# Attention into two expert layers: fills and first weight splits taken off GpSimd, and shorter block lookups

## The chip, the cores and the metric

The kernel runs on one core of one Trainium2 chip. The metric is the device time of one execution in microseconds (us). The five engines are named as in the profile: PE is TensorE's matmul and PEld its weight load, DVE is VectorE, ACT is ScalarE, POOL is GpSimd, and SP is the queue that issues most of the DMAs.

## The reference

Chunked attention (8 batches, 8 heads, 576 positions, chunks of 64), whose output is read as 4608 tokens of 512 numbers, then a layer of 8 experts that picks one expert per token, then a second layer of 8 experts with a capacity of 576 tokens each.

```python
def _attn_ref(q, k, v):
    scores = scale * np.matmul(q_c, k_c.transpose(0, 1, 2, 4, 3))
    scores = scores - np.max(scores, axis=-1, keepdims=True)
    attn = np.exp(scores)
    attn = attn / (np.sum(attn, axis=-1, keepdims=True) + 1e-09)
    out = np.matmul(attn, v_c)

def _moe_ref(x, w_gate, w_output_gate, w1, w2):
    e_idx = np.argmax(x @ w_gate, axis=1)
    for e in range(E):
        mask = e_idx == e
        h = np.maximum(x[mask] @ w1[e], 0.0)
        out[mask] = gate_w[mask, None] * eom[mask, e, None] * (h @ w2[e])
...
    x = _moe_ref(x=x, **moe_kwargs)
    return _moe2_ref(x=x, **moe2_kwargs)
```

## The kernel before, in words

The program has three stages that run into one another. The attention stage (`attention`) works through NT = 36 tiles of 128 tokens. Tile t needs one transfer pair `load_qkv(t)` into one of NQ = 7 buffers `qkv0` to `qkv6`, each half of which must hold zeros, because the two chunks of a tile share one block-diagonal matmul; `blanks` writes those zeros once, before the first load into a buffer. For each tile, `scores` makes 16 small matmuls (L412), takes the row maximum `mx` on DVE (L416) and scales it to `nm` (L419); `exps` makes 8 ACT instructions (L426); `probs_T` transposes on PE (L433) and evicts on ACT (`eT`, L435); `values` makes 16 matmuls into `O` (L448), and DVE divides by the row sums (`rs`, `x`, L450 to L458). `x_T` and `logits` feed the gate of the first expert layer (`xT`, L470, and L479).

Every four tiles, the gate's logits of a group of 512 tokens are ready, and a generator `route(g)` (L494 to L600) is queued. It is a chain of some 25 short DVE steps with a little PE and ACT work: it finds each token's expert and its rank among the tokens of that expert, and looks up in a table `tab` [expert, block] which block of 256 slots holds that rank. The lookup is `jd`, `ge`, `lk`, `te` and `slot` (L564 to L589), over all NJ = 18 possible blocks of all 8 experts: `lk` is 4 x 18 x 8 = 576 elements per partition. Four indirect DMAs on POOL (L594) then scatter the tokens into a list. `advance` takes steps of the oldest route at fixed places between the attention's own instructions (9 steps per tile), so the route's DVE steps lie in the same in-order queue as `mx`, `nm`, `rs` and `x`. For groups 3, 4 and 5 the route is followed by `early`, some 15 more short DVE steps that choose a first block of the expert layer.

The order on PE, DVE, ACT and SP is the order in which the code issues; POOL's order is the scheduler's. At the start, DVE and POOL fill the first buffers, POOL makes the constants (`ident`, several iotas), then POOL fills the remaining buffers 4 to 6 (L388, L389) and 13 working tiles (L328). From tile T0 = 23 on, at every second tile, SP fetches one of four chunks of the first expert's weights into `raw[c]` (`wr`), and from T1 = 24 on POOL splits it into a rounded part `whi` (L368) and a rest `wlo` (L369), 1024 elements per partition each. Later splits, of all other weights, are made by `split` on ACT (`whi`, L711) and DVE (`wlo`, L712).

The second stage is the jobs of the first expert layer (256 to 512 tokens each, `layer1`, `layer2`), the third the second layer (`moe2`). The rest of the routes of the last groups is taken between the matmuls of the first two jobs.

Of the kernel before, what the change touches and what calls it, by code (L numbers as in the profile page):

```python
# [8 lines left out]
F32 = mybir.dt.float32  # L9
# [4 lines left out]
AF = mybir.ActivationFunctionType  # L14
OP = mybir.AluOpType
# [13 lines left out]
E = 8  # L29
F = 1024  # L30
NT = N // 128
G = 4
NG = NT // G
BT = 256
NB = (N + E * (BT - 1)) // BT
NJ = N // BT
# [24 lines left out]
T0, T1, T2 = 23, 24, 28  # L61
# [11 lines left out]
class Kernel:  # L73
# [5 lines left out]
    def constants(self):  # L79
# [35 lines left out]
        self.wgs = c.tile([128, 4, 32], F32, name="wgs")  # L115
        nc.vector.memset(self.wgs, 0.0)
        nc.scalar.dma_start(self.wgs[:, :, 0:2 * E], self.wg)
        self.wg2s = c.tile([128, 4, 32], F32, name="wg2s")
        nc.vector.memset(self.wg2s, 0.0)
        nc.scalar.dma_start(self.wg2s[:, :, 0:E], self.wg2)  # L120
# [90 lines left out]
    def setup(self, st):  # L211
# [29 lines left out]
        self.tab = fix.tile([128, E, NJ], F32, name="tab")  # L241
# [59 lines left out]
    def attention(self, st):  # L301
# [7 lines left out]
        self.blanks(0, nc.vector, nc.gpsimd)  # L309
        self.load_qkv(0)  # L310
        self.blanks(1, nc.gpsimd, nc.vector)
# [4 lines left out]
        spare = self.wk.tile([128, 1], F32, name="spare", bufs=1)  # L316
        nc.vector.memset(spare, 0.0)
        nc.scalar.activation(spare, spare, AF.Exp)
        self.constants()
        for i in range(4, NQ):  # L320
            self.blanks(i, nc.gpsimd, nc.gpsimd)
            if i < LOOK:
                self.load_qkv(i)
        opened, total, acc = self.opened0, self.total0, self.acc0
        self.state = (acc, opened, total)
        for a, v in ((self.tab, 0.0), (self.order, 0.0), (opened, 0.0), (total, 0.0), (acc, 0.0),
                     (self.L, 0.0), (self.blank, 0.0), (self.left, E * (E - 1) / 2), (self.C, 0.0), (self.first, 0.0), (self.m, -BIG), (self.f, -BIG), (self.dead, -BIG)):
            nc.gpsimd.memset(a, v)  # L328
# [8 lines left out]
        for t in range(NT):  # L337
# [48 lines left out]
    def blanks(self, i, left, right):  # L386
        a = self.qkvb[i]
        right.memset(a[:, QKV:], 0.0)  # L388
        left.memset(a[:, 0:QKV - 512], 0.0)  # L389
# [108 lines left out]
    def route(self, g, lg):  # L498
# [64 lines left out]
        jd = wk.tile([128, G, NJ], F32, name="jd")  # L563
# [896 lines left out]
```

## Time and profile before

| quantity | value |
|---|---|
| time, median of 3 runs | 1234.52 us (1226.85 to 1237.56) |
| the profiled execution, its own time | 1218.32 us |
| its span in the trace | 1216.5 us |
| PE busy | 1106.5 us (91%) |
| DVE busy | 780.2 us (64%) |
| ACT busy | 489.5 us (40%) |
| POOL busy | 201.2 us (17%) |

The busy shares are means over stages with different limits. The attention stage fills about the first 185 us; the first expert layer goes on to about 730 us. The profiled execution is faster than each of the three runs shown. A busy PE in this table is also a slow PE: its granted clock has two levels, 1.2 and 2.4 GHz, which views by stretch show as a mean between 0.5 and 1.0.

### The profile page before, as it was taken

How to read it: one execution, taken by the hardware profiler on the slowest of the kernel's cores; microseconds unless marked ns; L12 is line 12 of the kernel's file. 1: busy time of each engine (PE TensorE's matmuls, PEld its weight loads, DVE VectorE, ACT ScalarE, POOL GpSimd, SP SyncE). 2: the span in 40 equal slices, each digit the busy share in tenths (PEclk: the TensorE clock that was granted, in tenths of full speed). 3: DMA queues.
4: the chain of work that ended last, by engine and by line, in shares of the span. 5: the costliest groups of instructions: out<-in, count | busy, mean ns of one | idle time of the engine just before them, and what ended most of it. 6: DMA issues, size and time to landing. Idle time of an engine off the chain costs nothing.

```text
span 1216.5 us, 23354 instructions
## 1 busy us (share of the span) xinstructions
PE 1106.5 (91%) x8424; PEld 968.1 (80%) x8424; DVE 780.2 (64%) x2214; ACT 489.5 (40%) x1052; POOL 201.2 (17%) x242
## 2 busy tenths in 40 slices
PE   5988779899999997999899628999999999999997
PEld 4766559897898997999889618787878787889795
DVE  5867877865356455666666677778878787843330
ACT  4766645444244333444445304233333333333331
POOL 6022442211101110010001010122120212221101
PEclk9999989899999999999999857999999999999999
DMA  6977846785464566576677523243333334342401
GB/s 235 302 206 214 300 117 164 165 243 168 117 181 130 174 191 188 139 220 193 189 237 219 167 62 120 91 131 116 106 127 96 126 96 126 107 147 108 169 10 39
DMA packets 90554, 189.67 MB, mean 156 GB/s; under 512 B 22992, under 2 KB 46608, under 8 KB 90384
## 3 DMA queue, kind: packets, MB, share of 16 engines
q1 hardware_dynamic: 77904, 153.96, 42.6%
q0 software_dynamic: 11136, 32.59, 8.6%
q8 instruction: 77, 1.26, 0.4%
q10 hardware_dynamic: 1344, 1.10, 0.3%
q14 instruction: 93, 0.76, 0.2%
HBM read 152.33 MB, written 35.28 MB: 154 GB/s over the span
## 4 chain that ended last, share of the span: by engine, by line
PE 53%; issue 13%; DVE 7%; DMA 5%; POOL 2%; ACT 1%; SPq 1%; POOLq 0%; DVEq 0%; ACTq 0%
PE ph L879 6%; PE O L879 6%; PE ph L1326 4%; PE ph L1328 4%; PE ph L1330 4%; PE py L1363 3%; PE py L1361 3%; PE py L1365 3%; PE ph L902 2%; PE ph L904 2%; PE ph L903 2%; PE py L1348 2%; PE O L902 2%; PE O L903 2%; PE O L904 2%
## 5 line engine op out<-in xcount | busy, mean ns | idle before, releaser
L712 DVE TENSOR_TENSOR wlo<-wr,whi 128x1024 fp32r<-128x1024 f32 x122 | 146.8, 1222 | 43.0 <-ACT whi L711 41.3
L1326 PE MATMUL ph<-xhi,whi 128*128 128x256 f32 (+1 forms) x512 | 155.0, 303 | 3.6 <-ACT xhi L1296 2.6
L711 ACT ACTIVATE whi<-wr 128x1024 fp32r<-128x1024 f32 x122 | 126.0, 1054 | 76.1 <-DMA wr<-in_w_dram 39.6
L1328 PE MATMUL ph<-xlo,whi 128*128 128x256 f32 (+1 forms) x512 | 154.0, 301 | 0.0
L1330 PE MATMUL ph<-xhi,wlo 128*128 128x256 f32 (+1 forms) x512 | 153.9, 301 | 0.0
L853 POOL DMA_INDIRECT xr<-xs,idx x48 | 48.1, 1003 | 401.4 <-DVE idx L851 160.9
L1363 PE MATMUL py<-wlo,hhi 128*128 128x512 f32 x256 | 105.3, 411 | 0.0
L1334 ACT ACTIVATE hhi<-ph 128x256 fp32r<-128x256 f32 x128 | 49.1, 384 | 135.5 <-PE ph L1330 133.8
L1365 PE MATMUL py<-whi,hlo 128*128 128x512 f32 x256 | 103.0, 402 | 0.0
L1361 PE MATMUL py<-whi,hhi 128*128 128x512 f32 x256 | 102.7, 401 | 0.0
L1326 PEld LDWEIGHTS ph<-xhi,whi 128*128 128x128 f32 x512 | 98.0, 191 | 5.3 <-ACT xhi L1296 3.3
L1328 PEld LDWEIGHTS ph<-xlo,whi 128*128 128x128 f32 x512 | 98.0, 191 | 0.4 <-DVE xlo L1297 0.2
L1330 PEld LDWEIGHTS ph<-xhi,wlo 128*128 128x128 f32 x512 | 97.8, 191 | 0.0
L1282 DVE TENSOR_TENSOR wlo<-wr,whi 128x512 fp32r<-128x512 f32 x124 | 82.1, 685 | 8.4 <-ACT whi L1277 8.4
L1335 DVE SCALAR_TENSOR_TENSOR hlo<-ph,hhi 128x256 fp32r<-128x256 f32 x128 | 52.9, 420 | 49.6 <-ACT hhi L1334 30.6
L879 PE MATMUL O<-xhi,whi 128*128 128x256 f32 (+4 forms) x240 | 75.6, 318 | 7.1 <-issue 7.1
L879 PE MATMUL ph<-xhi,whi 128*128 128x256 f32 (+4 forms) x240 | 74.6, 317 | 3.6 <-issue 2.1
L426 ACT ACTIVATE ex<-ph,nm 128x64 f32<-128x64 f32 x288 | 68.5, 352 | 22.3 <-DVE mx L416 13.5
L879 PE MATMUL O<-xhi,wlo 128*128 128x256 f32 (+4 forms) x240 | 74.2, 313 | 0.4 <-issue 0.4
L879 PE MATMUL ph<-xhi,wlo 128*128 128x256 f32 (+4 forms) x240 | 73.1, 310 | 0.0
L879 PE MATMUL O<-xlo,whi 128*128 128x256 f32 (+4 forms) x240 | 71.2, 314 | 0.2 <-issue 0.2
L879 PE MATMUL ph<-xlo,whi 128*128 128x256 f32 (+4 forms) x240 | 68.8, 313 | 1.7 <-issue 1.7
(326 smaller groups left out, 2752.8 us busy)
## 6 DMA issues: line engine op xcount, KB each, us to landing
wr<-in_w_dram SPq DMA_DIRECT2D x128, 512.0 KB
qkv<-in_qkv_dram SPq DMA_DIRECT2D x72, 386.0 KB
wr<-in_w2b_dram SPq DMA_DIRECT2D x32, 512.0 KB
wr<-in_w1b_dram SPq DMA_DIRECT2D x30, 512.0 KB
x<-y SPq DMA_DIRECT2D x184, 64.0 KB
xs<-x SPq DMA_DIRECT2D x35, 256.0 KB
x<-blank SPq DMA_DIRECT2D x8, 514.0 KB
wr<-in_w1b_dram ACTq DMA_DIRECT2D x2, 512.0 KB
```

Source lines behind the costliest of these rows:

```text
L426: self.nc.scalar.activation(ex8[:, h // 2, h % 2, :], S8[:, h, :], AF.Exp, scale=0.125, bias=nm[:, h:h + 1])
L711: nc.scalar.activation(hi, self.raw[c], AF.Copy)
L712: (eng or nc.vector).tensor_tensor(lo, self.raw[c], hi.bitcast(F32), op=OP.subtract)
L879: nc.tensor.matmul(p[:, q, :], a[:, k, :], b[:, k, 0:w], start=c == 0, stop=c == 11)
L1282: self.nc.vector.tensor_tensor(lo[:, s], self.raw[c][:, s], hi[:, s].bitcast(F32), op=OP.subtract)
L1326: nc.tensor.matmul(p, whi[:, k, :], xhi[:, k, cs], start=k == 0, stop=False)
L1328: nc.tensor.matmul(p, whi[:, k, :], xlo[:, k, cs], start=False, stop=False)
L1330: nc.tensor.matmul(p, wlo[:, k, :], xhi[:, k, cs], start=False, stop=k == 3)
L1335: self.later.append([LAG, lambda f=f, cs=cs, q=q: nc.vector.scalar_tensor_tensor(hlo[:, f, cs], q, 0.0, hhi[:, f, cs].bitcast(F32), op0=OP ...
L1361: nc.tensor.matmul(p, hhi[:, f, ts], whi, start=f == 0, stop=False)
L1363: nc.tensor.matmul(p, hhi[:, f, ts], wlo, start=False, stop=False)
L1365: nc.tensor.matmul(p, hlo[:, f, ts], whi, start=False, stop=f == 7)
```

## The change

Four things change. (1) The zeros of buffer 4 and the 13 working tiles are written by DVE, those of buffers 5 and 6 by ACT (as a copy of a zero), all before the first `mx` in program order; POOL keeps its part of buffers 0 to 3 and the constants. (2) The two small gate weights `wgs` and `wg2s` are loaded by SP's queue instead of ACT's. (3) The first four weight splits are made by ACT (`whi`, one instruction of 1024 at the end of tiles 25, 27, 29 and 31) and DVE (`wlo`, two halves of 512, at the ends of tiles 26 to 33) instead of POOL. (4) The lookup of group g covers n = 2 (g + 1) blocks instead of 18, since ranks of the first g + 1 groups reach no farther, and `tab` is stored as [block, expert], so that `lk` reads it in order while the update of `tab` and the steps of `early` read it with a stride.

```diff
-T0, T1, T2 = 23, 24, 28
+T0, T1, T2 = 23, 25, 28
...
-        self.tab = fix.tile([128, E, NJ], F32, name="tab")
+        self.tabT = fix.tile([128, NJ, E], F32, name="tab")
+        self.tab = self.tabT.rearrange("p j e -> p e j")
...
-        self.constants()
-        for i in range(4, NQ):
-            self.blanks(i, nc.gpsimd, nc.gpsimd)
-            if i < LOOK:
-                self.load_qkv(i)
-        for a, v in ((self.tab, 0.0), (self.order, 0.0), (opened, 0.0), (total, 0.0), (acc, 0.0),
-            nc.gpsimd.memset(a, v)
+        def clear(a, v):
+            nc.scalar.activation(a, spare[:, 0:1].to_broadcast(a.shape), AF.Copy)
+        for i in range(5, NQ):
+            self.blanks(i, clear, clear)
+        self.gates_w()
+        self.blanks(4, nc.vector.memset, nc.vector.memset)
+        for i in range(4, LOOK):
+            self.load_qkv(i)
+        for a, v in ((acc, 0.0), (opened, 0.0), (total, 0.0), (self.tabT, 0.0), (self.order, 0.0), (self.left, E * (E - 1) / 2),
+            nc.vector.memset(a, v)
+        self.constants()
...
             c, odd = divmod(t - T1, 2)
             if 0 <= c < 4 and not odd:
-                hi, lo = self.chunks[c]
-                nc.gpsimd.tensor_copy(hi, self.raw[c])
-                nc.gpsimd.tensor_tensor(lo, self.raw[c], hi.bitcast(F32), op=OP.subtract)
+                nc.scalar.activation(self.chunks[c][0], self.raw[c], AF.Copy)
+            c, h = divmod(t - T1 - 1, 2)
+            if 0 <= c < 4:
+                hi, lo = (a[:, h * CH // 2:(h + 1) * CH // 2] for a in self.chunks[c])
+                nc.vector.tensor_tensor(lo, self.raw[c][:, h * CH // 2:(h + 1) * CH // 2], hi.bitcast(F32), op=OP.subtract)
...
+    def gates_w(self):
+        nc = self.nc
+        for name, w, n in (("wgs", self.wg, 2 * E), ("wg2s", self.wg2, E)):
+            a = self.consts.tile([128, 4, 32], F32, name=name)
+            nc.vector.memset(a, 0.0)
+            nc.sync.dma_start(a[:, :, 0:n], w)
+            setattr(self, name, a)
...
-        jd = wk.tile([128, G, NJ], F32, name="jd")
+        n = min(NJ, G * 128 // BT * (g + 1))
+        jd = wk.tile([128, G, n], F32, name="jd")
...
-        sl = [128, G, NJ, E]
+        sl = [128, G, n, E]
         V.tensor_tensor(lk, oh[:, :, None, :].to_broadcast(sl),
-                        tab.rearrange("p e j -> p j e")[:, None, :, :].to_broadcast(sl), op=OP.mult)
+                        self.tabT[:, None, 0:n, :].to_broadcast(sl), op=OP.mult)
```

The order on DVE before the first `mx` of the program. `tri`, `ones` and `sel` are constants, `spare` a scratch column. Before:

```order
L389 MEMSET qkv_123 128x1032
L388 MEMSET qkv_124 128x1032
L317 MEMSET spare 128x1
L88 TENSOR_SCALAR tri<-jp 128x128
L90 MEMSET ones 128x128
L116 MEMSET wgs 128x128
L119 MEMSET wg2s 128x128
L122 TENSOR_REDUCE sel<-ident 128x32
L416 TENSOR_REDUCE mx<-ph 128x8
L419 TENSOR_SCALAR nm<-mx 128x8
```

The same place on DVE with the change, its last rows (`L`, `blank`, `C` and `first` are four of the 13 working tiles):

```order
L328 MEMSET L 128x400
L328 MEMSET blank 128x514
L328 MEMSET C 128x224
L328 MEMSET first 128x448
L88 TENSOR_SCALAR tri<-jp 128x128
L90 MEMSET ones 128x128
L116 TENSOR_REDUCE sel<-ident 128x32
L427 TENSOR_REDUCE mx<-ph 128x8
L430 TENSOR_SCALAR nm<-mx 128x8
```

Fifteen fills (two of buffer 4, 13 tiles) now stand ahead of `tri` on DVE; on POOL nothing but iotas and a few small fills follows the constants.

The order on POOL between the list scatters of groups 4 and 5 (`xr` is the gather of the first job's tokens). Before:

```order
L594 DMA list<-xm,idx 6400x2 x4
L368 CAST whi_85<-wr_81 128x1024
L369 TENSOR_TENSOR wlo_86<-wr_81,whi_85 128x1024
L506 COPY xm<-tokid 128x4
L368 CAST whi_87<-wr_82 128x1024
L853 DMA xr<-xs,idx 128x512
L369 TENSOR_TENSOR wlo_88<-wr_82,whi_87 128x1024
L853 DMA xr<-xs,idx 128x512
L594 DMA list<-xm,idx 6400x2 x4
```

The same place on POOL with the change:

```order
L606 DMA list<-xm,idx 6400x2 x4
L517 COPY xm<-tokid 128x4
L866 DMA xr<-xs,idx 128x512 x2
L606 DMA list<-xm,idx 6400x2 x4
L517 COPY xm<-tokid 128x4
```

All four pairs of cast and subtraction are gone from POOL (the other two stood behind the next copy of `xm`).

The order on DVE in the route of group 5 (tiles 28 and 29). Before:

```order
L452 RECIPROCAL rs<-rs 128x8
L575 TENSOR_SCALAR gzs<-gzs 128x4
L578 TENSOR_TENSOR lk<-roh,tab 128x576
L458 TENSOR_TENSOR x<-O,rs 128x256 x2
L581 SCALAR_TENSOR_TENSOR gzs<-gzs 128x4
L583 TENSOR_REDUCE te<-lk 128x72
```

The same place on DVE with the change, and the end of that tile:

```order
L463 RECIPROCAL rs<-rs 128x8
L587 TENSOR_SCALAR gzs<-gzs 128x4
L590 TENSOR_TENSOR lk<-roh,tab 128x384
L469 TENSOR_TENSOR x<-O,rs 128x256 x2
L593 SCALAR_TENSOR_TENSOR gzs<-gzs 128x4
L595 TENSOR_REDUCE te<-lk 128x48
...
L626 TENSOR_SCALAR pk<-pk,sd 128x24
L372 TENSOR_TENSOR wlo_88<-wr_82,whi_87 128x512
L427 TENSOR_REDUCE mx<-ph 128x8
```

`lk` stays ahead of `x` and shrinks from 576 to 384 elements; half a `wlo` comes in ahead of the next tile's `mx`.

The order on ACT at the end of tile 25, with the change (before, the `whi` row is not there):

```order
L481 ACTIVATE xT<-tp_2223 128x512
L368 ACTIVATE whi_85<-wr_81 128x1024
L437 ACTIVATE ex<-ph,nm 128x64 x4
L446 ACTIVATE eT<-tp_2262 128x512
L437 ACTIVATE ex<-ph,nm 128x64 x4
```

The `whi` of a chunk now stands in ACT's queue ahead of the exponentials of a later tile.

## Rows read from the trace of the kernel before

**Rows 1.** Windows, three stretches: busy us of each engine, granted clock, DMA share, GB/s.
```profile
30.00:45.00 15.00, 15.00 (x206) 12.16 (x204) 10.90 (x58) 11.87 (x44) 0.00 (x0) 1.00 0.95 312
...
135.00:150.00 15.00, 11.74 (x158) 9.34 (x158) 13.07 (x48) 8.58 (x34) 10.87 (x9) 1.00 0.87 288
...
165.00:180.00 15.00, 10.69 (x114) 8.09 (x111) 11.84 (x38) 7.01 (x24) 7.85 (x7) 0.89 0.54 129
```
**Rows 2.** Timeline of the start: start us, duration us, engine, line, operation, wait before it.
```profile
7.45 1.98 PE L412 MATMUL ph<-qkv 128*64 128x128 f32 x16 [7.45 <-DVE wgs L116]
...
10.19 6.58 DVE L419 TENSOR_SCALAR nm<-mx 128x8 f32<-128x8 f32 x1
...
10.26 1.97 PE L412 MATMUL ph<-qkv 128*64 128x128 f32 x16 [0.83 <-DVE mx L416]
...
12.26 4.51 DVE L416 TENSOR_REDUCE mx<-ph 128x8 f32<-128x512 f32 x1
...
16.83 0.17 DVE L419 TENSOR_SCALAR nm<-mx 128x8 f32<-128x8 f32 x1
16.87 2.58 ACT L426 ACTIVATE ex<-ph,nm 128x64 f32<-128x64 f32 x12 [13.48 <-DVE mx L416]
...
19.08 1.98 PE L412 MATMUL ph<-qkv 128*64 128x128 f32 x16
```
**Rows 3.** Timeline, POOL: the first and last of 19 fills that follow one another.
```profile
8.46 0.95 POOL L388 MEMSET qkv<- 128x1032 f32 x1
...
16.52 0.13 POOL L328 MEMSET dead<- 128x50 f32 x1
```
**Rows 4.** By line: a fill on DVE (mean ns), a copy on ACT (min/median/max ns).
```profile
L389 DVE MEMSET qkv<- 128x1032 f32 x1 | 0.9, 918 | 1.1 <-PEq L1448 1.1
...
L711 ACT ACTIVATE whi<-wr x122: 1043/1052/1064, 191.5 to 731.8; 128x1024 fp32r<-128x1024 f32 x122
```
**Rows 5.** By line, lookup and a subtraction of 512: min/median/max ns, first and last start.
```profile
L578 DVE TENSOR_TENSOR lk<-roh,tab x9: 1119/1147/1204, 52.9 to 214.5; 128x576 f32<-128x576 bf16 x9
L583 DVE TENSOR_REDUCE te<-lk x9: 736/746/755, 54.7 to 215.8; 128x72 f32<-128x576 f32 x9
...
L1282 DVE TENSOR_TENSOR wlo<-wr,whi x124: 678/684/739, 740.2 to 1179.1; 128x512 fp32r<-128x512 f32 x124
```
**Rows 6.** By line: POOL's subtraction and four DVE steps of the route, min/median/max ns.
```profile
L369 POOL TENSOR_TENSOR wlo<-wr,whi x4: 2357/2364/2378, 138.5 to 167.3; 128x1024 fp32r<-128x1024 f32 x4
...
L566 DVE SCALAR_TENSOR_TENSOR cm<-cs,jlo x9: 301/303/3184, 51.6 to 213.5; 128x144 f32<-128x144 f32 x9
L553 DVE TENSOR_TENSOR new<-opened x8: 293/304/2341, 68.0 to 212.6; 128x144 f32<-128x144 f32 x8
L533 DVE TENSOR_TENSOR gz<-lg,roh x9: 136/142/1982, 48.5 to 209.3; 128x32 f32<-128x32 f32 x9
L522 DVE TENSOR_TENSOR roh<-rw,rf x9: 181/182/1037, 47.9 to 203.3; 128x32 bf16<-128x32 f32 x9
```
**Rows 7.** Timeline, PE rows that waited for DVE: start, duration, wait in brackets.
```profile
54.53 1.11 PE L448 MATMUL O<-qkv,eT 128*64 128x130 f32 x16 [0.24 <-DVE x L458]
...
135.54 1.11 PE L448 MATMUL O<-qkv,eT 128*64 128x130 f32 x16 [1.75 <-DVE x L458]
...
151.53 1.11 PE L448 MATMUL O<-qkv,eT 128*64 128x130 f32 x16 [3.29 <-DVE x L458]
...
163.92 0.18 PE L528 MATMUL tp<-roh,tri 128*128 128x32 bf16 x1 [1.40 <-DVE roh L522]
...
173.91 2.00 PE L448 MATMUL O<-qkv,eT 128*64 128x130 f32 x16 [3.98 <-DVE x L458]
```
**Rows 8.** Timeline: first fetch of a chunk, ACT's place two tiles later, a later wait.
```profile
124.16 0.85 SPq L705 DMA_DIRECT2D wr<-in_w_dram  x1
...
131.91 0.60 ACT L470 ACTIVATE xT<-tp 128x512 f32<-128x512 f32 x1 [1.17 <-PE tp L468]
...
235.88 1.06 ACT L711 ACTIVATE whi<-wr 128x1024 fp32r<-128x1024 f32 x1 [5.55 <-DMA wr<-in_w_dram]
```

More of the change, by code (lines that the diff above doesn't have):

```diff
@@ L114, in constants @@
                        allow_small_or_imprecise_dtypes=True)
[L115 to L120, printed above, removed]
         self.sel = c.tile([128, 32], F32, name="sel")
@@ L308, in attention @@
             self.qkvb.append(a)
-        self.blanks(0, nc.vector, nc.gpsimd)
+        opened, total, acc = self.opened0, self.total0, self.acc0
+        self.state = (acc, opened, total)
+        self.blanks(0, nc.vector.memset, nc.gpsimd.memset)
         self.load_qkv(0)
-        self.blanks(1, nc.gpsimd, nc.vector)
+        self.blanks(1, nc.gpsimd.memset, nc.vector.memset)
         self.load_qkv(1)
         for i in (2, 3):
-            self.blanks(i, nc.gpsimd, nc.gpsimd)
+            self.blanks(i, nc.gpsimd.memset, nc.gpsimd.memset)
             self.load_qkv(i)
-        spare = self.wk.tile([128, 1], F32, name="spare", bufs=1)
+        spare = self.wk.tile([128, 2], F32, name="spare", bufs=1)
         nc.vector.memset(spare, 0.0)
-        nc.scalar.activation(spare, spare, AF.Exp)
-        self.constants()
-        for i in range(4, NQ):
-            self.blanks(i, nc.gpsimd, nc.gpsimd)
-            if i < LOOK:
-                self.load_qkv(i)
-        opened, total, acc = self.opened0, self.total0, self.acc0
-        self.state = (acc, opened, total)
-        for a, v in ((self.tab, 0.0), (self.order, 0.0), (opened, 0.0), (total, 0.0), (acc, 0.0),
-                     (self.L, 0.0), (self.blank, 0.0), (self.left, E * (E - 1) / 2), (self.C, 0.0), (self.first, 0.0), (self.m, -BIG), (self.f, -BIG), (self.dead, -BIG)):
-            nc.gpsimd.memset(a, v)
+        nc.scalar.activation(spare[:, 1:], spare[:, 1:], AF.Exp)
+        def clear(a, v):
[7 more added lines that the diff above has]
+        for a, v in ((acc, 0.0), (opened, 0.0), (total, 0.0), (self.tabT, 0.0), (self.order, 0.0), (self.left, E * (E - 1) / 2),
+                     (self.m, -BIG), (self.f, -BIG), (self.dead, -BIG), (self.L, 0.0), (self.blank, 0.0), (self.C, 0.0),
+                     (self.first, 0.0)):
+            nc.vector.memset(a, v)
+        self.constants()
         self.xp = {}
@@ L387, in blanks @@
         a = self.qkvb[i]
-        right.memset(a[:, QKV:], 0.0)
-        left.memset(a[:, 0:QKV - 512], 0.0)
+        right(a[:, QKV:], 0.0)
+        left(a[:, 0:QKV - 512], 0.0)
+    def gates_w(self):
[5 more added lines that the diff above has]
+            setattr(self, name, a)
     def finish(self, i):
@@ L562, in route @@
         yield
-        jd = wk.tile([128, G, NJ], F32, name="jd")
-        V.tensor_tensor(jd, rank[:, :, None].to_broadcast([128, G, NJ]), self.jthr, op=OP.subtract)
+        n = min(NJ, G * 128 // BT * (g + 1))
+        jd = wk.tile([128, G, n], F32, name="jd")
+        V.tensor_tensor(jd, rank[:, :, None].to_broadcast([128, G, n]), self.jthr[:, :, 0:n], op=OP.subtract)
         cm = wk.tile(sj, F32, name="cm")
@@ L567, in route @@
         yield
-        ge = wk.tile([128, G, NJ], F32, name="ge")
+        ge = wk.tile([128, G, n], F32, name="ge")
         V.tensor_scalar(ge, jd, 0.0, None, op0=OP.is_ge)
@@ L628, in plan @@
     def plan(self, cnt, used):
-        V, wk, tab = self.nc.vector, self.wk, self.tab
+        V, wk = self.nc.vector, self.wk
         sj = [128, E, NJ]
+        tab = wk.tile(sj, F32, name="ptab", bufs=1)
         jf = "p e j -> p (e j)"
@@ L633, in plan @@
         V.tensor_tensor(d, cnt[:, :, None].to_broadcast(sj), self.jlo, op=OP.subtract)
-        V.tensor_tensor(tab, tab, self.jlo, op=OP.add)
+        V.tensor_tensor(tab, self.tab, self.jlo, op=OP.add)
         V.tensor_scalar(tab, tab, 1.0 / BT, None, op0=OP.mult)
```

2 lines of the change are left out of this document (1 added, 1 removed).

## The prediction
> **What bounds the kernel now.** Read the page first, then the windows of the attention stage, then its timeline, then the rows by line. The page says that PE bounds the whole, but the change touches only the first 185 us or so, and there the windows tell another story [rows 1]. At 30 to 45 us, before the first route, PE is busy all 15 us. At 135 to 150 it is busy 11.7 of 15 and DVE 13.1; at 165 to 180 PE 10.7 and DVE 11.8. So from the first route on it is DVE that PE waits for, and the timeline names where: the O matmuls wait for `x`, the rank matmuls for `roh` [rows 7]. At the very start neither works: `nm`, an instruction on 8 numbers per partition, starts at 10.19 and lasts 6.58 us; the same operation takes 0.17 us at 16.83 [rows 2]. Everything behind it (exponentials, transposes, the next scores) waits.
>
> The profiled execution took 1218.32 us, 1.8 us more than its span; the three runs have a median of 1234.52, 1.3% above it. I work out a difference in the profiled execution and take it off the median, since no term depends on what lies between the two.
>
> **The start.** `nm` ends at 16.77, 0.1 us after the last of POOL's 19 fills (16.65) [rows 2, 3], though it reads only `mx` and needs nothing of POOL. I take POOL's run of fills for the cause. The change leaves POOL none of these fills. What is then late next: the second scores, which PE runs from 10.26 to 12.23, as before, because that is when the second tile is there. `mx` of the second tile takes some 0.7 us (the second `mx` ended with the stall, and without it is an `mx` like any other; as an estimate, the 0.69 us that the line for 512 elements below gives), `nm` 0.17, so its exponentials start near 13.2. In the old trace they are the last 4 of 12 that start at 16.87 and take 2.58 us, so they began near 18.6. The stage starts 5.4 us earlier by that; the third scores, at 19.08 before, follow at about 14. I take **-5.0**. Bounds: -6.5, the whole stall, and -4.0, if the tiles land more slowly. Tile 0 is used at 7.45, tile 1 at 10.26: 2.8 us apart, which puts tile 2 at 13.1 against a need at 14; at 3.4 us apart a later tile would be a microsecond late.
>
> What is added to the start has cover. DVE's own fill of 1032 elements takes 0.92 us [rows 4]; two of them, the 13 tiles (2.8 us on POOL: from 13.9, after six fills of about 0.9 us from 8.46, to 16.65 [rows 3]) and five constants of at most 128 elements (0.3 us each, as an estimate by the line below) make some 6.1 us after DVE's first two fills, which begin at 1.1 and end near 3.0: done near 9.1, before the first scores end at 9.43 [rows 2]. If they ran 1 us longer, the start would lose up to that. ACT's four copies of 1032 take 4 x 1.05 us [rows 4] and are done long before its first exponential. The two gate-weight loads go ahead of tile 4 in SP's queue; they are a few per cent of a tile's bytes, and I cost them at nothing.
>
> **The lookups.** One DVE instruction on 144 elements takes 0.304 us (`new`) and one on 512 takes 0.684 [rows 5, 6]: 0.155 us plus 1.03 ns per element. Over nine groups the lookup has 64 to 576 elements, 320 on the mean. `lk`: 9 x (1.147 - 0.485) = 6.0 us less. `te`: 9 x 256 x 1.03 ns = 2.4 less. Five steps on 72 elements lose 32 elements each on the mean, 45 x 0.033 = 1.5 less. Against it, `tab` is now updated with a stride. By the line, 576 elements in order would take 0.75, `lk` with its strided table takes 1.147, so a strided operand costs about 0.7 ns per element; two such on 144 elements are 0.2 us, nine times 1.8: I take half, 0.9. In all 9.0 us less DVE work.
>
> The Trainium skill (Vector Engine (DVE) Microarchitecture Reference, section Measured stream behaviour on trn2) speaks against this part of the change in one point: a port that steps by single words runs at 1.7 to 2.5 ns per column instead of 1.05, and a strided destination pays as a source does. By it the update of `tab` would take up to 0.43 us, 1.2 us more over nine, and `lk` in order 0.41 us on the mean, 0.7 us less over nine than by my line; the two nearly cancel. That `lk` pays for its stride the trace confirms (1.147 against 0.75).
>
> What of the 9.0 us is on the path: in groups 0 to 2 PE waits for `x` by 0.24 us once per group [rows 7], so -0.7. In groups 3 to 5, with `early` behind the route, PE waited 1.75 us at 135 [rows 7], more than a group saves: -1.2, -1.0 and -0.8 for n = 8, 10 and 12 (`lk` and `te` alone 1.06, 0.92 and 0.79). Group 6 lies in a wait that the next part removes: -0.3. Groups 7 and 8 run beside the jobs, where PE does not wait for a lookup: 0. I take **-4.0**; bounds -9.0 and -1.5.
>
> **The splits leave POOL.** POOL's subtraction takes 2.36 us, four times between 138.5 and 170. Four DVE steps, each with one slow instance among nine, are at their longest 3.18, 2.34, 1.98 and 1.04 us, against medians of 0.30, 0.30, 0.14 and 0.18 [rows 6]: 7.6 us lost. PE's waits for DVE in that stretch are 3.29, 1.40 and 3.98, together 8.7 us [rows 7]. They have one cause by size and place. I take **-8.0**; bounds -8.7 and -6.0, since a DVE that is freed meets other waits.
>
> **The splits arrive on DVE and ACT.** DVE: 8 x 0.684 = 5.5 us [rows 5], one in each of tiles 26 to 33, ahead of the next `mx`. DVE is about full there, but after the two parts above it has 8 to 10 us more room in this stretch. I take **+3.5**, between 0 and 5.5. ACT: 4 x 1.05 = 4.2 us, ahead of exponentials; ACT is busy 8.6 and 7.0 of 15 us [rows 1], so most is hidden: **+1.0**, between 0 and 4.2. The granted clock of 0.89 at 165 to 180 shows PE at half speed for a while after its long wait; the O matmuls at 173.91 take 2.00 us instead of 1.11. That may go too: 0, down to -2.
>
> **Sum:** -5.0 - 4.0 - 8.0 + 3.5 + 1.0 = **-12.5 us**. The profiled execution would take 1205.8, the median 1222.0. The jobs and the second layer are untouched, and start earlier by what attention gives.
>
> **Rivals.** (a) *DVE stays the bound, and the new splits are paid in full.* For it: DVE busy 13.1 of 15 us. Against it: the room of 8 to 10 us that the other parts make in the same stretch. Then lookups -1.5, splits +5.5, copies +4.2: -5.0 - 1.5 - 8.0 + 5.5 + 4.2 = -4.8, 1229.7. (b) *The start is not POOL's doing*, and 6.58 us stay, as something else holds `nm`. Against it: the end within 0.1 us of the last fill. Then -7.5, 1227.0. (c) *All of DVE's saved work counts*, and the clock stays up: with the new splits at 2.5, under half: -6.5 - 9.0 - 8.7 + 2.5 - 2 = -23.7, 1210.8. For it: DVE is in order and nearly full. Against it: PE alone needs most of each tile. (d) *Slower: ACT waits for the chunk.* `whi` stands in ACT's queue two tiles after its fetch, and exponentials are queued behind it. The fetch left at 124.16, ACT's place was about 132: 8 us. Landing later than that stops ACT, `eT`, O and so the whole stage, four times. After 8 us each microsecond costs 4; from 11 us on the gain is gone, at 15 us per landing it is +28 - 12.5 = +15, 1250. For it: later in the trace ACT does wait 5.55 us for a chunk [rows 8], and the DMA share is 0.87 to 0.95 here [rows 1]. Against it: that later wait is behind many fetches at once, here one chunk goes beside the tiles.
>
> **How the numbers follow.** Forecast 0.50, (a) 0.23, (b) 0.08, (c) 0.14, (d) 0.05. A difference of 1%, 12.3 us, is about what a measurement of this kernel tells from none; the forecast lies on that edge, so about 0.6 of its chance, and all of (c), goes to faster beyond 1%, with a little of (a)'s spread: 0.47. Slower is (d) with little else: 0.05. The rest, 0.48, is within 1%. The range reaches from (c) to a little beyond (a): 1210 to 1232; the forecast's own is 1217 to 1227.
>
> **What would show it.** Right: the first `nm` at 0.17 us near 10.2, the third scores near 14; no DVE step of the route over 0.6 us between 120 and 175; `lk` from about 0.2 us in group 0 to 0.75 in group 8; the O matmuls that stood at 173.91 come near 161; the jobs as long as before. Wrong: an early `nm` but scores that wait for tiles; ACT idle in front of `whi` with a DMA as releaser; PE's waits for `x` as long as before with half splits ahead of them; or a gain at 170 that is gone where the first jobs start.

## The result, and the profile after

The changed kernel took a median of 1213.57 us (4 runs, 1210.73 to 1215.77) beside 1231.03 us for the kernel before (4 runs): a ratio of 0.9882, 95% interval 0.9834 to 0.9931 (ratios are estimated over all runs of both kernels; the two medians alone would give 0.9858). The forecast, 1222.0 on 1234.52, is a ratio of 0.9899. In a second comparison on another chip (9 runs against 22) the ratio was 0.9922, 0.9896 to 0.9948. Both intervals hold the forecast's ratio, and both are wide, because runs of one kernel on one chip differ by up to 16 us. The two profiled executions are 1218.32 and 1215.32 us, only 3 us apart; the one of before was faster than all its other runs, and no trace shows where those lose their 8.5 to 19 us. The traces therefore say where time moved inside an execution; only the ratios say how much came out.

The timeline of the start of the changed kernel (PE, DVE, ACT; start, duration, what was done, wait in brackets), to be read beside [rows 2]:

```profile
6.91 1.97 PE L423 MATMUL ph<-qkv 128*64 128x128 f32 x16 [6.91 <-DMA qkv<-in_qkv_dram]
12.48 1.47 PE L423 MATMUL ph<-qkv 128*64 128x128 f32 x16
15.07 1.09 PE L423 MATMUL ph<-qkv 128*64 128x128 f32 x16
...
9.65 0.33 DVE L430 TENSOR_SCALAR nm<-mx 128x8 f32<-128x8 f32 x1
...
10.07 1.75 ACT L437 ACTIVATE ex<-ph,nm 128x64 f32<-128x64 f32 x8 [2.87 <-DVE nm L430]
```

`nm` takes 0.33 us instead of 6.58. The first exponentials start at 10.07 instead of 16.87. The third scores come at 12.48 instead of 19.08, and take 1.47 us, the fourth 1.09. The `nm` of tile 4 (counted from 1) moves from 24.56 to 17.01 and that of tile 12 from 51.87 to 44.30: 7.6 us.

By line, in the changed kernel (min/median/max ns, first and last start; for `whi` also what ACT waited for), beside [rows 5, 6]:

```profile
L590 DVE TENSOR_TENSOR lk<-roh,tab x9: 215/492/759, 45.4 to 201.4; 128x64 f32<-128x64 bf16 x1, 128x128 f32<-128x128 bf16 x1, 128x192 f32<-128x192 bf16 x1, 128x256 f32<-128x256 bf16 x1
L595 DVE TENSOR_REDUCE te<-lk x9: 206/478/753, 46.3 to 202.1; 128x8 f32<-128x64 f32 x1, 128x16 f32<-128x128 f32 x1, 128x24 f32<-128x192 f32 x1, 128x32 f32<-128x256 f32 x1
L585 DVE TENSOR_TENSOR tab<-tab,cm x9: 417/433/451, 44.9 to 200.9; 128x144 f32<-128x144 f32 x9
L578 DVE SCALAR_TENSOR_TENSOR cm<-cs,jlo x9: 299/301/303, 44.1 to 200.2; 128x144 f32<-128x144 f32 x9
L368 ACT ACTIVATE whi<-wr x4: 1039/1045/1060, 118.1 to 149.4; 128x1024 fp32r<-128x1024 f32 x4
its engine sat idle before it (us, times) until:
  DMA wr<-in_w_dram: 0.6, 1
```

`lk` runs from 0.22 to 0.76 us with the number of blocks. The update of `tab` costs 0.43 us. `cm`, which had one instance of 3.18 us, has a maximum of 0.30, and the other three steps of [rows 6] one of 0.31 at most. From the slopes that the Trainium skill (Vector Engine (DVE) Microarchitecture Reference, section Measured stream behaviour on trn2) states, the prediction had estimated up to 0.43 us for the strided update, where my line gave about 0.4; the measured median is 0.433, so the trace agrees with the page. For `lk` in order the estimate from the same section was 0.41 us on the mean, and my line gave 0.485; the measured median is 0.492, so there the line was right and the estimate too low.

PE's timeline at the end of attention and in the first expert jobs, beside [rows 7]; two rows of the kernel before, then the changed kernel:

```profile
187.52 0.39 PE L879 MATMUL ph<-xhi,whi 128*128 128x256 f32 x1
...
232.30 1.12 PE L859 MATMUL tp<-ident,xr 128*128 128x128 f32 x4 [3.36 <-DMA xr<-xs,idx]
```
```profile
144.92 1.11 PE L459 MATMUL O<-qkv,eT 128*64 128x130 f32 x16 [2.06 <-DVE rs L463]
...
159.74 1.11 PE L459 MATMUL O<-qkv,eT 128*64 128x130 f32 x16 [1.11 <-DVE x L469]
168.55 1.11 PE L479 MATMUL tp<-ident,x 128*128 128x128 f32 x4 [2.81 <-DVE gex L525]
174.01 0.39 PE L892 MATMUL ph<-xhi,whi 128*128 128x256 f32 x1
...
223.25 1.11 PE L872 MATMUL tp<-ident,xr 128*128 128x128 f32 x4 [8.48 <-DMA xr<-xs,idx]
```

Of the waits of 1.40 to 3.98 us for DVE there remain 2.06, 1.11 and 2.81. The first expert matmul comes at 174.01; before it was at 187.52, so attention gives 13.5 us in this pair of traces. But PE then waits 8.48 us for the gathered tokens of job 2 (jobs are counted from 0), 3.36 in the kernel before. The windows of 200 to 240 us, before and then after (columns as in [rows 1], PEld behind PE):

```profile
200.00:240.00 40.00, 35.96 (x282) 34.80 (x282) 36.09 (x105) 17.56 (x27) 10.57 (x10) 0.91 0.72 168
```
```profile
200.00:240.00 40.00, 31.25 (x246) 30.28 (x248) 27.65 (x79) 13.44 (x20) 12.10 (x10) 0.87 0.72 182
```

PE is busy 4.7 us less, at a lower clock (0.87 against 0.91). Beside the same part of the work in the kernel before, 213.5 to 253.5, it is 4.4 us less (35.62 us there, clock 0.91). The second layer's first matmul is only 6.3 us earlier (725.7 against 732.0). POOL's timeline, and one row of DVE's, show what stood before that gather:

```profile
207.68 1.13 POOL L606 DMA_INDIRECT list<-xm,idx  x1 [13.71 <-DMA meta<-list]
...
212.98 3.09 POOL L866 DMA_INDIRECT xr<-xs,idx  x1 [0.30 <-issue]
...
212.84 2.35 DVE L725 TENSOR_TENSOR wlo<-wr,whi 128x1024 fp32r<-128x1024 f32 x2
```

The last group's list scatters on POOL waited until 207.68 for SP's read of the list (`meta`, L857, issued at 201.57 at the start of job 1); their own indices were written by 203.62. The gather of job 2 (L866) stands behind them. Its first half lasts 3.09 us on POOL, where most take about 1.0: it starts just after DVE has begun two subtractions of 1024, and ends 0.88 us after the second of them.

### The profile page after: what moved, and what is told of

It is laid out like the page before. It is cut to its first block, busy times and chain, and to the rows that moved or that the text cites. A ratio compares the mean times of both kernels' runs of the same rounds, so it can differ in the third digit from the quotient of the medians.

```text
span 1213.5 us, 23360 instructions
## 1 busy us (share of the span) xinstructions
PE 1111.6 (92%) x8424; PEld 975.6 (80%) x8424; DVE 766.5 (63%) x2237; ACT 496.4 (41%) x1060; POOL 184.1 (15%) x215
## 3 DMA queue, kind: packets, MB, share of 16 engines
q10 hardware_dynamic: 288, 1.05, 0.3%
## 4 chain that ended last, share of the span: by engine, by line
PE 57%; issue 11%; DVE 7%; DMA 4%; POOL 2%; ACT 1%; SPq 0%; POOLq 0%; DVEq 0%; ACTq 0%
PE O L892 7%; PE ph L892 7%; PE ph L1339 4%; PE ph L1343 4%; PE ph L1341 4%; PE py L1376 3%; PE py L1374 3%; PE py L1378 3%; PE ph L917 2%; PE ph L915 2%; PE ph L916 2%; PE O L915 2%; PE O L917 2%; PE O L916 2%; PE py L1361 2%
## 5 line engine op out<-in xcount | busy, mean ns | idle before, releaser
L725 DVE TENSOR_TENSOR wlo<-wr,whi 128x1024 fp32r<-128x1024 f32 x122 | 146.7, 1222 | 40.2 <-ACT whi L724 38.7
L866 POOL DMA_INDIRECT xr<-xs,idx x48 | 50.1, 1044 | 406.0 <-DVE tp L794 112.7
```

The source lines that it names most:

```text
L725: (eng or nc.vector).tensor_tensor(lo, self.raw[c], hi.bitcast(F32), op=OP.subtract)
```

## The experiments

The kernels ran on three chips, whose kernel before had medians of 1208.93, 1207.95 and 1214.93 us; each ratio is to the kernel before on the same chip. Landmarks are in us, from one profiled execution each; none was taken of the kernel before on these chips. Ten kernels share the new start, and their `nm` of tile 12 lies between 43.9 and 45.3: up to there a landmark is good to about 1.5 us. Later ones are not. The two traces of the changed kernel, on two chips, have the `nm` of tile 36 at 157.5 and 150.8 and the first expert matmul at 174.0 and 162.9. And "fetch first" with and without the early list read, which on one chip do the same work in the same order up to the `nm` of tile 36, differ there by 4.2 us and at the first expert matmul by 4.8. So at these two landmarks a difference of under 5 us between two traces shows nothing by itself. "Gap" is the time from the first expert matmul to PE's first transposition of job 2's tokens, "wait" what PE waited for these.

| kernel | ratio to before, 95% | nm of tile 36 | first expert matmul | gap | wait | second layer |
|---|---|---|---|---|---|---|
| start only | 0.9936 (0.9909 to 0.9963) | 157.3 | 171.8 | 45.5 | 5.2 | 720.5 |
| all but the start | 0.9969 (0.9942 to 0.9996) | 158.2 | 170.3 | 49.7 | 9.3 | 720.1 |
| full lookup | 0.9884 (0.9846 to 0.9921) | 152.7 | 165.1 | 48.7 | 8.4 | 712.7 |
| splits on POOL | 0.9893 (0.9857 to 0.9930) | 148.1 | 167.5 | 45.1 | 4.8 | 711.9 |
| changed kernel again | 0.9922 (0.9896 to 0.9948) | 150.8 | 162.9 | 45.3 | 5.0 | 711.6 |
| fills given back to POOL | 0.9954 (0.9924 to 0.9984) | 153.2 | 165.3 | 49.3 | 9.0 | 721.7 |
| list read early | 0.9887 (0.9858 to 0.9917) | 150.4 | 162.4 | 45.3 | 4.9 | 706.8 |
| half splits twice | 0.9940 (0.9913 to 0.9967) | 150.5 | 163.3 | 48.8 | 8.4 | 707.6 |
| fetch first | 0.9914 (0.9879 to 0.9948) | 151.2 | 163.3 | 50.5 | 10.0 | 721.4 |
| fetch first, list read early | 0.9886 (0.9846 to 0.9927) | 155.4 | 168.1 | 45.7 | 5.4 | 713.9 |
| fetch first, half splits twice | 0.9915 (0.9883 to 0.9947) | 154.2 | 167.0 | 50.7 | 10.4 | 720.4 |
| fetch first, full lookup | 0.9915 (0.9887 to 0.9944) | 155.3 | 167.7 | 51.1 | 9.9 | 721.2 |

**Start only, and all but the start.** The kernel before with parts 1 and 2 of the change, and the changed kernel with these two undone.

> The kernel before with the new start alone (parts 1 and 2 of the change). Theory: POOL's fills held the first nm, and the 7.5 us that the changed kernel has gained at tile 11 (nm at 44.3 instead of 51.9) is the start's alone. Then the first nm takes under 0.4 us, tile 11's nm stands near 44.3, the last tile's near 164 (171.3 less 7.5), and the time is some 7 us below the kernel before. Rival: the start's gain is eaten in the stretch where DVE is full, so the last nm stands at 168 or later and the time is within 4 us of before.

> The changed kernel with the old start (fills on POOL, gate weights on ACT's queue). Theory: the first nm stalls about 6.5 us again until POOL's last fill ends; the last nm stands near 165 (157.5 plus 7.5), the time 5 to 8 us above the changed kernel. Rival: later waits absorb a late start, so the time is within 3 us of the changed kernel.

The start alone is worth 0.64%, 7.7 us. All the rest without it is worth 0.31%, 3.7 us. With the start alone the first `nm` takes 0.17 us, and that of tile 12 (tile 11 in the expectation, counted from 0 there) comes at 45.3. Without the new start it comes at 53.1, and the first `nm` stalls again, for longer than before (DVE, then POOL):

```profile
10.21 8.22 DVE L422 TENSOR_SCALAR nm<-mx 128x8 f32<-128x8 f32 x1
...
16.51 0.13 POOL L329 MEMSET dead<- 128x50 f32 x1
...
18.20 0.20 POOL L203 MEMSET mem<- 128x129 bf16 x1
```

I had expected it to end with the last of POOL's 19 fills, at 16.64. It ended 1.8 us later, at 18.43, while POOL ran on through iotas and small fills of constants, 0.03 us after one of these (`mem`). In the kernel before, `nm` was let go at 16.77 in the same run of POOL's work. So more than the 19 fills can hold it, and what lets it go is not shown.

The last `nm` came at 157.3 and 158.2, not near 164 and 165. Those figures were counted from the changed kernel's first trace; beside its second one (150.8) they are 6.5 and 7.4 us late. At the first expert matmul, against the same second trace, the start gives 7.4 us (170.3 against 162.9) and the rest 8.9 (171.8 against 162.9), but beside the first trace (174.0) neither would give anything. Tile 12 and the ratio carry the start's gain: it arrives in the time whole, as far as its interval of 3.3 us to either side can tell. Of the rest, 3.7 us arrive, with an interval of 0.5 to 7.0.

**Full lookup, and splits on POOL.** The changed kernel with one part undone each. In the first the table stays stored as [block, expert], so `lk` takes 0.76 us in every group, not 1.15 as before the change.

```diff
-        n = min(NJ, G * 128 // BT * (g + 1))
+        n = NJ
```
```diff
-T0, T1, T2 = 23, 25, 28
+T0, T1, T2 = 23, 24, 28
...
-                nc.scalar.activation(self.chunks[c][0], self.raw[c], AF.Copy)
...
+                hi, lo = self.chunks[c]
+                nc.gpsimd.tensor_copy(hi, self.raw[c])
+                nc.gpsimd.tensor_tensor(lo, self.raw[c], hi.bitcast(F32), op=OP.subtract)
```

> The changed kernel with the lookup over all 18 blocks in every group, the table still stored as [block, expert]. Theory: lk at 0.76 us and te at 0.75 in all nine groups, 5 to 6 us more DVE work, of which a part lies on PE's path: the last nm 1 to 3 us later than 157.5, the time 1 to 4 us above the changed kernel. Rival: DVE is no longer the bound once POOL's subtractions are gone, and neither moves by more than 1 us.

> The changed kernel with the four first splits back on POOL. Theory: two-input DVE steps of the route stall behind POOL's subtractions again, four or more of them by 1 to 3 us, and the last nm stands 3 to 6 us later than 157.5 although DVE has 5.5 us and ACT 4.2 us less to do. Rival: the splits on DVE and ACT cost what the stalls cost, and the last nm stays within 1.5 us of 157.5.

Neither is slower than the changed kernel by a measurable amount: 0.9884 and 0.9893 beside its 0.9882 and 0.9922. But both are shorter than the start alone on the same chip (0.9936; medians 1194.39 and 1194.76 us against 1202.96), by 6.3 and 5.2 us, with intervals that just overlap. Both parts together bring 1.7 to 6.5 us over the start. So either part alone seems to bring what both bring: their gains do not add. (The kernel with the full lookup still reads its table in order, so some of that part's gain stays in it.) At the first expert matmul the two kernels are 2.2 and 4.6 us later than the changed kernel's second trace, at the `nm` of tile 36 1.9 us later and 2.7 us earlier; that is within the spread of traces. The 3 to 6 us that I expected with the splits on POOL did not come. In the kernel with the splits on POOL the stalls are back (timeline of DVE, then POOL, then PE):

```profile
128.18 3.21 DVE L580 SCALAR_TENSOR_TENSOR cm<-cm,new 128x144 f32<-128x144 f32 x1
148.07 2.31 DVE L428 TENSOR_SCALAR nm<-mx 128x8 f32<-128x8 f32 x1
151.51 2.35 DVE L582 SCALAR_TENSOR_TENSOR ge<-jd,ge 128x56 f32<-128x56 f32 x1
...
128.84 2.36 POOL L370 TENSOR_TENSOR wlo<-wr,whi 128x1024 fp32r<-128x1024 f32 x1
147.94 2.41 POOL L370 TENSOR_TENSOR wlo<-wr,whi 128x1024 fp32r<-128x1024 f32 x1
151.41 2.38 POOL L370 TENSOR_TENSOR wlo<-wr,whi 128x1024 fp32r<-128x1024 f32 x1
...
155.33 2.00 PE L457 MATMUL O<-qkv,eT 128*64 128x130 f32 x16 [6.66 <-DVE x L467]
```

Three steps of other kinds, one of them `nm` on 8 numbers, end within 0.2 us of the end of POOL's subtraction: 131.39 and 131.20, 150.38 and 150.35, 153.86 and 153.79. (A fourth, not shown, does so at 120.96 and 120.91.) PE waits 6.66 us for DVE there, and its next O matmuls run at half speed (2.00 us). This is the prediction's cause, seen a second time.

**Fills given back to POOL.** Four fills of 1024 elements and one of 2048 on POOL behind its constants, into buffers that nobody reads then.

```diff
+        for a in (*self.raw, self.xr):
+            nc.gpsimd.memset(a, 0.0)
```

> The changed kernel with six us or so of fills given back to POOL behind its constants: of the four weight buffers and the gather's buffer, 6 x 1024 elements per partition, which nobody reads then. DVE, ACT and all transfers stay as they are. If POOL's run of fills is what held the first nm, that instruction lasts 4 to 7 us again and ends within 0.2 us of the last of these fills; tiles 4 and 12 have their nm 4 to 7 us later than in the changed kernel, and the time is 4 to 7 us longer. Rival: the stall came from the fills of buffers 4 to 6, that is from tiles that arrived late behind them, or from the gate weights on ACT's queue. Then nm stays at 0.2 to 0.4 us and the time within 1 us of the changed kernel.

```profile
8.46 3.62 POOL L331 MEMSET wr<- 128x1024 f32 x4
10.95 2.91 DVE L432 TENSOR_SCALAR nm<-mx 128x8 f32<-128x8 f32 x1
12.03 1.79 POOL L331 MEMSET xr<- 128x2048 f32 x1
13.92 1.05 DVE L432 TENSOR_SCALAR nm<-mx 128x8 f32<-128x8 f32 x1
```

The timeline of POOL and DVE shows `nm` at 2.91 us. It ends at 13.86, POOL's last fill at 13.82. The stall is shorter than expected, since the fills began 2.5 us ahead of `nm`. The second `nm` lasts 1.05 us too, while POOL runs iotas. The `nm` of tiles 4 and 12 come 3.6 and 3.7 us later than in the changed kernel on the same chip (I had expected 4 to 7), and the median is 4.5 us longer (1202.35 against 1197.84), with intervals that overlap. POOL's fills alone bring the stall back, with DVE, ACT and all transfers as in the changed kernel; the rival, late tiles, falls.

**Changed kernel again, and half splits twice.** The second doubles one line of the change.

```diff
                 nc.vector.tensor_tensor(lo, self.raw[c][:, h * CH // 2:(h + 1) * CH // 2], hi.bitcast(F32), op=OP.subtract)
+                nc.vector.tensor_tensor(lo, self.raw[c][:, h * CH // 2:(h + 1) * CH // 2], hi.bitcast(F32), op=OP.subtract)
```

> The changed kernel itself, on the chip of the other runs, as their common yardstick. If the parts add up as I summed them, it stands at 0.985 to 0.988 of the kernel before, that is about as far below the kernel with the change of the start alone (0.9936) as lookups and splits together were to bring. If lookups and splits put back singly cost nothing because each alone already makes the room that the next wait allows, it stands where those two kernels stand, 0.987 to 0.990, and its first expert layer starts within 2 us of theirs (165.1 and 167.5).

> The changed kernel with each of the eight half subtractions of the first four splits made twice: 8 x 0.68 = 5.5 us more work on DVE in tiles 26 to 33, nothing else. If DVE bounds that stretch (my prediction costed the eight at 3.5 us on the path), the nm of tile 36 and the first weight load of the expert layer come 3 to 5.5 us later and the time is 3 to 5 us longer. If there is room on DVE by now, as the kernel with the splits back on POOL suggests, they come under 1.5 us later and the time stays within 1 us.

The changed kernel again stands at 0.9922, above both ranges that I had given for it. The doubled work cost nothing by the `nm` of tile 36 (150.5 against 150.8) and 0.4 us at the first expert matmul; its median is 3.4 us longer (1201.24 against 1197.84), within intervals that overlap. The trace of the changed kernel on this chip shows what may give DVE the room (SP, ACT, PE):

```profile
109.54 0.43 SPq L857 DMA_DIRECT2D meta<-list  x1
110.19 0.36 SPq L718 DMA_DIRECT2D wr<-in_w_dram  x1
114.77 0.78 SPq L718 DMA_DIRECT2D wr<-in_w_dram  x1
...
114.51 1.06 ACT L368 ACTIVATE whi<-wr 128x1024 fp32r<-128x1024 f32 x1 [7.22 <-DMA wr<-in_w_dram]
126.98 1.06 ACT L368 ACTIVATE whi<-wr 128x1024 fp32r<-128x1024 f32 x1 [3.19 <-DMA wr<-in_w_dram]
...
116.93 1.30 PE L444 MATMUL tp<-ident,ex 128*128 128x128 f32 x4 [6.53 <-ACT eT L446]
129.39 1.15 PE L444 MATMUL tp<-ident,ex 128*128 128x128 f32 x4 [2.05 <-ACT eT L446]
```

ACT waits 7.22 and 3.19 us for the first two chunks, and PE behind it 6.53 and 2.05. In the first trace of the same kernel this wait was 0.6 us in all. The fetch left only at 110.19, because SP's queue stood 7.6 us before the read at 109.54, which waited for a list scatter of POOL's.

**Fetch first.** The first chunk's fetch is issued ahead of that read.

```diff
                 self.open(0)
-                self.x_list(0)
             c, odd = divmod(t - T0, 2)
             if 0 <= c < 4 and not odd:
                 self.fetch(c, self.w1, self.reg)
+            if t == T0:
+                self.x_list(0)
```

> The changed kernel with the first weight fetch issued ahead of the first job's read of the list on SP, instead of behind it. In the changed kernel ACT waited 7.2 us for the first chunk and 3.2 us for the second, since that read waited 7.6 us for a scatter of POOL's and the fetch stood behind it; PE waited 6.5 and 2.1 us for ACT. If that queue order is the cause, ACT's wait for the first chunk falls under 1 us, PE has no wait over 2 us between 105 and 125 us, the nm of tile 36 comes 4 to 7 us earlier (near 145) and the time falls by 2 to 6 us. Rival: the chunk itself is slow to land, or the tiles' loads behind the read are the bound. Then the fetch leaves near 102 but ACT or PE waits as long in total, and the nm of tile 36 moves by less than 2 us.

```profile
102.71 0.36 SPq L719 DMA_DIRECT2D wr<-in_w_dram  x1
111.21 0.41 SPq L858 DMA_DIRECT2D meta<-list  x1
115.61 0.35 SPq L719 DMA_DIRECT2D wr<-in_w_dram  x1
...
112.13 1.06 ACT L369 ACTIVATE whi<-wr 128x1024 fp32r<-128x1024 f32 x1 [2.11 <-DMA wr<-in_w_dram]
126.58 1.06 ACT L369 ACTIVATE whi<-wr 128x1024 fp32r<-128x1024 f32 x1 [6.47 <-DMA wr<-in_w_dram]
```

The fetch leaves 7.5 us earlier and ACT's first wait falls to 2.11 us; but the first chunk now takes 9.4 us from issue to use, and the second waits 6.47. In all ACT waits 8.6 instead of 10.4 us, and neither the `nm` of tile 36 nor the time (0.9914 beside 0.9922) moves. With the same order and the early list read below, ACT waited for all four chunks, 13.5 us in all: the wait differs from one execution to the next by more than this edit changes. The queue order was a cause of the first wait but not the bound: the rival holds. From issue to use a chunk took 4.3 us after SP had stood still (110.19 to 114.51), and 9.4 to 12.2 us in the other cases; two tiles from fetch to use are too few for that. A later place for `whi` was not tried.

**Fetch first with half splits twice, and with the full lookup.** Each is two of the edits above together.

> The fetch ahead of the list's read, and each half subtraction made twice (5.5 us more on DVE in tiles 26 to 33). With the chunk's wait there the doubled work cost nothing by the nm of tile 36 (150.5 against 150.8). If it was hidden in the room that this wait gave DVE, it now costs 2 to 5 us at the nm of tile 36 against the kernel with the fetch first alone. If DVE has room of its own in these tiles, it again costs under 1 us.

> The fetch ahead of the list's read, and the lookup over all 18 blocks again, as before the change. With the chunk's wait there the full lookup cost 1.9 us at the nm of tile 36 and 2.2 us at the first weight load of the expert layer. If that wait had hidden the lookup's price, it now costs 3 to 5 us at both places against the kernel with the fetch first alone (my prediction said 4.0). If the shortened lookup buys room that nobody uses, it costs under 2 us again.

Against the kernel with the fetch first alone, the first expert matmul is 3.7 and 4.4 us later, and the `nm` of tile 36 3.0 and 4.1. But the kernel with the fetch first and the early list read, which does the same work up to that `nm`, is later too, by 4.8 and 4.2 us at these two places. So these traces do not show that either edit costs anything. At tile 35, where those two kernels agree (147.1 and 146.7), the doubled splits stand at 149.4 and the full lookup at 151.2: a hint, from one trace each. Both medians are the same as without (1203.05 and 1204.90 against 1204.69): all three wait about 10 us for job 2's tokens, and what differs ahead of that does not show at the end.

**List read early.** Job 2's read of the list is moved from job 1's start to the last tile, once on the changed kernel and once with the fetch first. (The expectations call job 2 the second job.)

```diff
                 self.x_list(1)
+                self.x_list(2)
...
-            if 1 <= j < EARLY - 1:
-                self.x_list(n)
```

> The changed kernel with the second job's read of the list moved from the start of the first expert job to the last tile of attention, beside the first job's. If POOL's list scatters of the last group wait for that read (they waited 13.7 us for the list's reader in the changed kernel) and the gather of the second job's tokens waits behind them on POOL, then the scatter's wait falls to under 8 us, PE's wait for those tokens from 8.5 us to 2 to 5 us, and the time falls by 3 to 6 us. Rival: the gather is held by something else that ends at the same time (the scatter's own index, the transfer itself, DMA queues full of weights). Then PE's wait stays at 7 us or more and the time within 1 us.

> The fetch ahead of the list's first read, and the second job's read of the list beside the first job's: both edits that took a wait away, on the changed kernel. If they are worth what they seem singly, the expert layer starts near 158, and the time is 0.983 to 0.987 of the kernel before, the shortest of all. If the time after attention swallows what attention gives, it stands at 0.987 to 0.990, like the kernels that differ from it.

POOL, DVE and PE, with the fetch first and the read where it was:

```profile
197.87 1.11 POOL L607 DMA_INDIRECT list<-xm,idx  x1 [11.83 <-DMA meta<-list]
...
203.17 3.09 POOL L867 DMA_INDIRECT xr<-xs,idx  x1 [0.30 <-PE O L893]
...
203.03 2.35 DVE L726 TENSOR_TENSOR wlo<-wr,whi 128x1024 fp32r<-128x1024 f32 x2
...
213.78 1.12 PE L873 MATMUL tp<-ident,xr 128*128 128x128 f32 x4 [9.99 <-DMA xr<-xs,idx]
```
```profile
200.00:240.00 40.00, 30.01 (x233) 29.16 (x232) 25.13 (x63) 14.83 (x21) 10.26 (x9) 0.83 0.75 191
```

The same with the read early:

```profile
198.06 0.96 POOL L608 DMA_INDIRECT list<-xm,idx  x1 [8.32 <-DVE ptab L649]
...
204.05 0.98 POOL L866 DMA_INDIRECT xr<-xs,idx  x1 [0.30 <-issue]
...
206.52 2.35 DVE L727 TENSOR_TENSOR wlo<-wr,whi 128x1024 fp32r<-128x1024 f32 x2
...
213.82 1.12 PE L872 MATMUL tp<-ident,xr 128*128 128x128 f32 x4 [5.39 <-DMA xr<-xs,idx]
```
```profile
200.00:240.00 40.00, 34.61 (x274) 33.86 (x274) 28.34 (x73) 17.47 (x25) 8.94 (x9) 0.91 0.86 197
```

The scatter no longer waits for `meta`: counted from the first expert matmul it starts at 30.0 us instead of 34.6. The gather starts at 36.0 instead of 39.9, now ahead of DVE's pair of subtractions and not inside it, and takes 0.98 us on POOL instead of 3.09. PE's wait falls from 9.99 to 5.39 us. The window shows 34.6 us of busy PE instead of 30.0, and a clock of 0.91 instead of 0.83. On the changed kernel itself the one trace had a short wait already (5.0), so there the edit shows in the ratio alone: 0.9887 against 0.9922, here 0.9886 against 0.9914. Both point the same way, by 4.2 and 3.4 us; each pair of intervals overlaps. The scatter's wait was expected under 8 us and was 9.1 and 8.3; it ended with other work of the route. With both edits the expert layer was to start near 158; it started at 168.1, and the time is the one I had given if the time after attention swallows what attention gives (0.987 to 0.990).

The table's gaps fall in two groups, 45.1 to 45.7 and 48.7 to 51.1. The kernel before has 44.8, the first trace of the changed kernel 49.2. In the first group the gather's first half takes 1.0 us on POOL, in the second 2.4 to 3.1. In every trace of the second it starts while DVE is in that pair of subtractions, in every trace of the first it is over before they start. In the fourteen traces 76 indirect DMAs on POOL in the first 650 us last over 1.2 us, and each of them ends 0.82 to 0.93 us after a two-input DVE step (`wlo` or `lk`) that ran when it started, or after the one right behind that. No run moved these subtractions alone. Over the six executions of the first group (with the kernel before) the time from the first expert matmul to the second layer is 544.4 to 548.7 us, mean 546; over the eight of the second 544.3 to 558.1, mean 552; the shortest of all is in the second, so the gap decides only part of that time. No kernel was shown to be shorter than the changed one beyond its interval; the early read is the best candidate.

## Why the prediction was right, and where not

The sign and the size held: 1213.57 lies inside the range of 1210 to 1232, and the forecast's ratio inside both intervals. Step by step:

- **The start**, "I take **-5.0**": the mechanism was right (fills on POOL hold `nm`, shown by giving them back), the size too small: 7.6 us at tile 12 in the first pair of traces, 7.7 in the time of the start alone (4.5 to 11.0). I let the third scores follow at 14, behind the second tile's exponentials; they came at 12.48, right behind the first tile's transposes, which need only the first tile's. They and the next then took 1.47 and 1.09 us; the third had taken 1.98 before. Tiles were not late. That the stall ends with the fills was true of the kernel before and not of the one without the new start.
- **The lookups**, "I take **-4.0**": DVE's work fell as I had costed it (576 elements read in order take 0.76 us, by my line 0.75). In the time, the short lookup is worth about 5.2 us over the start alone with the splits on POOL, and nothing measurable with the splits moved. The readings at the first expert matmul (4.3 us, 2.2, and 4.4 with the fetch first) lie within the spread of traces.
- **The splits leave POOL, and arrive**, "**-8.0**" and "**+3.5**": the four long DVE steps are gone and come back with the splits on POOL. (One of the four in [rows 6], `roh`, ended with POOL's cast, not with a subtraction: at 163.87 and 163.82.) With ACT's +1.0 I had -3.5 in all; in the time it is about 6.3 us over the start alone with the full lookup, its table read in order, and nothing measurable with the short one. What the half splits cost DVE is not shown: doubling them moved neither time beyond its interval.
- **The sum** added the lookups and the splits as if each removed waits of its own. By the ratios they do not add: -7.5 in all was forecast behind the start, 1.7 to 6.5 us came. With a start that gave more than forecast, the total seems partly right by cancellation.
- **ACT's copies**, "most is hidden: **+1.0**": mis-sized, and by the mechanism of rival (d). ACT waited 10.4 us for chunks in one trace and 0.6 in another. Rival (d) fell as a forecast: the changed kernel is not slower, in its traces at most the first two of the four chunks wait, and the kernel with the splits on POOL, which has no such wait, is not measurably shorter.
- **"The jobs and the second layer are untouched, and start earlier by what attention gives"**: this step did not hold. In the first pair of traces they start 13.5 us earlier, but job 2's tokens do not come earlier by as much, and 7.2 us are given back by the time the second layer starts (in the second trace of the changed kernel that stretch takes 3.0 us less). I had named this as a sign of being wrong ("a gain at 170 that is gone where the first jobs start") but put no price on it.
- **Rivals.** (a) was a ratio of 0.9961 and (c) one of 0.9808: both lie outside both intervals. (b) falls with the start alone.

Three things stay open: which of the changed kernel's two ratios, 0.9882 and 0.9922, is nearer (their intervals overlap), why its two traces part by 11 us before the expert layer, and whether ACT's wait would go with a later `whi`.

## What to carry to other kernels

When an instruction on a handful of numbers lasts microseconds, look for the end that coincides with its own: here a run of GpSimd work, in every kernel that had it beside short DVE steps, and taking the fills off GpSimd was worth most of the change. Two parts that shorten the same stretch can each be worth something alone and no more together; measure each on top of the other before adding them. Before reading a few us off single traces, see how far two traces of one program differ. A gain in one stage should be followed to the next stage's first transfer: what is read, scattered and gathered through in-order queues does not come earlier because the engines do. Work that is moved to a queue two tiles behind a fetch needs the fetch's real latency under load, 4 to 12 us here, not the distance in the program.

## What the runs showed of the hardware that was not expected

DVE is held not only by POOL's two-input subtraction but by plain fills, and across several instructions. In the kernel before, `nm` (one input, 8 numbers) waited from 10.19 until 0.1 us after POOL's run of fills [rows 2, 3]; with the fills given back it waited through the last three, to within 0.04 us of their end; with all but the start it waited on through iotas, 1.8 us past the fills. The Trainium skill (SBUF — State Buffer, section Who interferes with whom) says that VectorE and GpSimd share a pair of ports, that a VectorE instruction in a two-port mode, which a `tensor_scalar` like `nm` can enter, contends with GpSimd for it, that whoever issues first has it "for the whole instruction", and that the other fully blocks. The traces agree on the block; but here it lasted over several POOL instructions, not one. Whether `nm` ran in such a mode no run shows.

The hold goes the other way, too. Of the indirect DMAs that POOL issues in the first 650 us, most last 0.94 to 1.2 us. The 76 that last longer all started while DVE was in a two-input step and ended 0.82 to 0.93 us after that one or the one right behind it; the longest, behind two subtractions of 1024, lasted 3.09 us. This rests on the coincidence of their ends; no run was made to test it.

A long wait of PE went with a lower clock behind it. Between the kernels with the late and the early list read the windows of 200 to 240 us differ by 4.6 us of busy PE, as the two waits do (9.99 and 5.39). The granted clock was 0.83 against 0.91; over 40 us that is, as an estimate, up to another 3.2 us of PE at 2.4 GHz. It is not so in every trace: the changed kernel's second one has 0.87 there, as the first, with a wait of 5.0 us against 8.5.
